# Scores taken chunk by chunk, banks held back for the next in line, and a finer clock in the planner of a linear-attention and mixing kernel

## The chip, the cores and the metric

The kernel runs on one core of one Trainium2 chip. The metric is the device time of one execution in microseconds (us). PE is the matrix engine, VectorE (DVE), ScalarE (ACT) and GpSimd (POOL) are the others. A profile is one execution; the times come from several. A quoted ratio is the mean time of one kernel's fast runs over the mean time of the fast runs of the kernel before in the same rounds, so it is not quite the ratio of the medians that stand beside it. The kernel before was timed again with every batch of experiments; its medians lay between 172.65 and 173.91 us. The changed kernel was timed once, beside the 172.69 us. So a difference in us between it and an experiment crosses batches between which the kernel before alone moved by up to 1.2 us; the ratios are the safer measure.

## The reference, cut to what matters

```python
# attention: batch 4, heads 8, sequence 768, head size 48
for t in range(S):
    cur = einsum('bhd,bhe->bhde', u * k[t], v[t])
    y[t] = einsum('bhd,bhde->bhe', r[t], state + cur)
    state = w * state + einsum('bhd,bhe->bhde', k[t], v[t])
# mixing: x is y with the heads joined, (4, 768, 384)
theta = x @ w_theta
y = einsum('ts,bsd->btd', w_tok_r, x * cos(theta)) + einsum('ts,bsd->btd', w_tok_i, x * sin(theta))
u = x + y
out = u + relu(u @ w_ch)
```

## The kernel before

The recurrence is done in chunks of 128 tokens, two chunks to a "pair", three pairs to a batch. Per pair, PE computes the scores of both chunks, VectorE masks them while it evicts them, PE forms the outputs; x, theta, sine and cosine follow. When all three pairs of a batch are there, the token mix runs: six outputs of 12 matmuls each, in four parts of three.

The kernel is not written in its final order. It declares tasks with their dependencies, engines and estimated durations, and a planner in the kernel lists them in the order of a simulated execution. The instructions are then issued in that order. Each piece of accumulator memory (PSUM) that a task needs is a token, and the planner also chooses its banks. There are 8 banks, and they are allocated as four tiles of two banks:

```python
    P = Plan(8)
    banks = [ps.tile([C, 2, 512], F32, name=f"bank{i}") for i in range(4)]

    def dbl(tok):                      # a token of two banks: a whole tile
        return banks[P.bank_of[tok] // 2]

    def bank(tok):                     # a token of one bank: half a tile
        i = P.bank_of[tok]
        return banks[i // 2][:, i % 2]
```

A token of one bank goes, if it can, beside a bank that is taken already, so that whole tiles stay free for tokens of two banks:

```python
    def pick_banks(self, acq, free, now):
        # ...
                i = min(avail, key=lambda i: ((i ^ 1) in avail, free[i]))
```

In the planner a task may start when its inputs are there, and a task's end includes a latency for the engine's pipeline, also for the next task on the same engine:

```python
                    t.end = now + ns + lat
                    # ...
                    for x in t.users:
                        x.ready = max(x.ready, t.end)
```

The token mix and its eviction, and the scores:

```python
        for t in range(2):
            to = 2 * pr + t
            tm = ("mx", b, to)
            for part in range(4):
                def mix(e, tm=tm, to=to, part=part):
                    # three matmuls into bank(tm)
                P.add({PE: pe_op(490)}, mix, ..., acq=[(tm, 1)] if part == 0 else [], ...)
            P.add({DVE: dve_op(HD)}, lambda e, ...: nc.vector.tensor_add(
                un[:, t], bank(tm)[:, :HD], x[:, to]), use=[tm], ...)
        flips(uT, [un[...] ...], ("TU", g), ...)      # six transposes on PE, then uT is evicted

        tk = [("A", g, hi) for hi in range(2)]
        # scores of both chunks: two double banks at once
        P.add({PE: pe_op(470)}, scores, rd=[kT] + rt_keys, acq=[(t, 2) for t in tk], ...)
```

## Time and profile before

| | before |
|---|---|
| median of the first 3 runs | 172.65 us (172.62 to 174.24) |
| span of the profiled run | 172.2 us |
| PE busy | 137.9 us, 80% |
| first transposes on PE | 8.80 us |
| first mixing matmul | 45.3 us |
| end of the last attention output | 138.9 us |
| mixing matmuls after that | 99 of 288 |

The page's first two parts, of the kernel before. The first line has each engine's busy time; the others are tenths of busy time and of granted clock in 40 equal slices of the span.

```profile
PE 137.9 (80%) x1491; PEld 96.1 (56%) x1491; DVE 113.2 (66%) x163; ACT 71.6 (42%) x102; POOL 76.2 (44%) x62
...
PE   3056699997969869968699999997899999699970
...
PEclk9999999999999999999969999999999999999995
```

The clock records of this run begin only at 28.47 us. Before that the row shows 9s because there is no record, not because the clock was full.

PE leads, with 34 us idle, some of it in the start and the last eviction, the rest in many short gaps.

### The profile page before, as it was taken

The numbers are of one execution on the slowest core, as the hardware profiler recorded it, in microseconds if no ns is written. First come the engines' busy times: TensorE is split into PE (matmuls) and PEld (weight loads), VectorE is DVE, ScalarE is ACT, GpSimd is POOL, SyncE is SP. The second block draws the span as 40 slices with busy tenths as digits, with TensorE's granted clock in tenths as the row PEclk, the third lists the DMA queues.
The fourth block names the chain that finished last, engine by engine and source line by source line (L and its number), as shares of the span: only waits on it lengthen the run. The fifth ranks groups of instructions, "written<-read, shape, count | busy, mean of one in ns | idle before, by whom it ended". The sixth has DMA issues, their size and how long they took to land.

```text
span 172.2 us, 3640 instructions
## 1 busy us (share of the span) xinstructions
PE 137.9 (80%) x1491; PEld 96.1 (56%) x1491; DVE 113.2 (66%) x163; ACT 71.6 (42%) x102; POOL 76.2 (44%) x62
## 2 busy tenths in 40 slices
PE   3056699997969869968699999997899999699970
PEld 1046568786745646646485657566656665455530
DVE  6274976963418897476888668646799885344361
ACT  3966236775953425457633532556105213000000
POOL 6003328079941507999799791330333332100000
PEclk9999999999999999999969999999999999999995
DMA  5999999999993399799999900220020022020222
GB/s 164 239 240 163 169 372 373 392 372 157 177 159 53 92 325 152 136 197 195 344 161 157 168 12 20 75 91 0 4 91 4 0 93 89 6 91 0 91 91 91
DMA packets 59962, 25.00 MB, mean 145 GB/s; under 512 B 50473, under 2 KB 58410, under 8 KB 59946
## 3 DMA queue, kind: packets, MB, share of 16 engines
q1 hardware_dynamic: 59920, 24.78, 65.7%
q8 instruction: 11, 0.18, 0.5%
q14 instruction: 5, 0.04, 0.1%
q10 hardware_dynamic: 26, 0.00, 0.0%
HBM read 20.06 MB, written 4.72 MB: 144 GB/s over the span
## 4 chain that ended last, share of the span: by engine, by line
PE 53%; DVE 21%; ACT 11%; issue 7%; DMA 3%; POOL 3%; ACTq 1%; DVEq 0%; POOLq 0%
PE bank L677 22%; PE bank L472 8%; PE bank L694 7%; PE bank L645 6%; DVE mAT L549 5%; ACT RT L260 5%; DVE un L683 3%; DMA wu<-in_u_dram 3%; PE bank L626 2%; DVE fin L698 2%; DVE uT L262 2%; POOL zi L658 2%; PE bank L543 2%; DVE xT L262 2%; DVE Sb L601 2%
## 5 line engine op out<-in xcount | busy, mean ns | idle before, releaser
L677 PE MATMUL bank<-zi,WiT 128*128 128x384 bf16 x144 | 29.9, 326 | 3.7 <-DVE Sb L607 1.4
L569 POOL TENSOR_TENSOR yd<-dg,vb 128x768 bf16<-128x768 f32 x12 | 17.6, 1473 | 33.1 <-ACT dg L260 33.1
L677 PE MATMUL bank<-zr,WrT 128*128 128x384 bf16 x144 | 29.6, 326 | 2.9 <-ACT RT L260 1.4
L658 POOL TENSOR_TENSOR zi<-x,sin 128x768 bf16<-128x768 bf16 x12 | 19.9, 1657 | 25.0 <-ACT sin L649 25.0
L549 DVE TENSOR_TENSOR mAT<-bank,mask 128x1024 bf16<-128x1024 f32 x24 | 29.0, 1216 | 1.0 <-PE bank L543 1.0
L519 POOL TENSOR_TENSOR Kw<-ld,wpinv 128x768 bf16<-128x768 f32 x11 | 19.8, 1822 | 11.7 <-ACT RT L260 11.7
L683 DVE TENSOR_TENSOR un<-bank,x 128x384 bf16<-128x384 f32 x24 | 13.2, 555 | 16.4 <-PE bank L677 9.4
L677 PEld LDWEIGHTS <-WiT 128*128 128x128 bf16 x144 | 13.3, 97 | 11.7 <-issue 4.6
L677 PEld LDWEIGHTS <-WrT 128*128 128x128 bf16 x144 | 13.1, 97 | 11.1 <-issue 4.2
L649 ACT ACTIVATE sin<-bank 128x768 bf16<-128x768 f32 x12 | 9.7, 811 | 20.5 <-DVE fin L698 10.6
L260 ACT ACTIVATE RT<-bank 128x768 bf16<-128x768 bf16 x16 | 12.8, 815 | 9.4 <-PE bank L472 5.5
L491 POOL TENSOR_TENSOR Rw<-r_f,wpow 128x576 bf16<-128x576 f32 x12 | 16.6, 1409 | 0.0
L698 DVE SCALAR_TENSOR_TENSOR fin<-bank,un 128x768 f32<-128x768 f32 x12 | 11.5, 956 | 6.5 <-PE bank L694 6.4
L645 PE MATMUL bank<-Wth,xT 128*128 128x384 bf16 x72 | 14.7, 343 | 1.2 <-DVE xT L262 0.9
L694 PE MATMUL bank<-Wch,uT 128*128 128x384 bf16 x72 | 13.7, 327 | 1.4 <-DVE uT L262 1.4
L633 DVE TENSOR_TENSOR x<-bank,yd 128x768 bf16<-128x768 f32 x12 | 11.4, 951 | 2.5 <-PE bank L626 1.3
L655 DVE TENSOR_TENSOR zr<-bank,x 128x768 bf16<-128x768 f32 x12 | 11.4, 950 | 1.1 <-ACT bank L652 1.1
L472 PE MATMUL bank<-ident,Rw 128*128 128x128 bf16 x96 | 8.9, 241 | 3.4 <-ACT RT L260 1.9
L260 ACT ACTIVATE vb<-ld 128x768 bf16<-128x768 f32 x12 | 10.1, 840 | 3.5 <-DMA ld<-in_v_dram 3.4
L260 ACT ACTIVATE KT<-bank 128x1024 bf16<-128x1024 bf16 x7 | 7.2, 1023 | 9.5 <-PE bank L677 4.0
L626 PE MATMUL bank<-vb,mAT 128*128 128x48 bf16 x192 | 9.6, 189 | 1.7 <-DVE mAT L549 1.6
L652 ACT ACTIVATE bank<-bank,pi 128x768 f32<-128x768 f32 x12 | 10.5, 875 | 0.0
(76 smaller groups left out, 212.3 us busy)
## 6 DMA issues: line engine op xcount, KB each, us to landing
ld<-in_k_dram SPq DMA_DIRECT2D x24, 192.0 KB, 5.3
ld<-in_v_dram SPq DMA_DIRECT2D x24, 192.0 KB, 5.2
out_dram<-fin SPq DMA_DIRECT2D x12, 384.0 KB, 2.5
r_f<-in_r_dram SPq DMA_DIRECT2D x3, 1152.0 KB, 7.8
ld<-in_moe_w_tok_r_dram SPq DMA_DIRECT2D x6, 384.0 KB, 8.6
ld<-in_moe_w_tok_i_dram SPq DMA_DIRECT2D x6, 384.0 KB, 8.2
r_f<-in_r_dram SPq DMA_DIRECT2D x2, 576.0 KB, 4.6
ld<-in_moe_w_theta_dram SPq DMA_DIRECT2D x1, 384.0 KB, 5.0
```

Of the source, the lines that this page charges most:

```text
L260: nc.scalar.activation(dst, src, Act.Copy)
L472: nc.tensor.matmul(bank16(tok)[:, i * C:(i + 1) * C], s, ident, is_transpose=True, start=(i == 0), stop=(i == n - 1))
L491: eng_of[e].tensor_mul(Rw[:, :, 2 * hp:2 * hp + 2, :D].transpose([0, 2, 1, 3]), rf[:, 2 * hp:2 * hp + 2, :].rearrange("p h (n d) -> p h n ...
L519: eng_of[e].tensor_mul(Kw[:, :, :, :D].rearrange("p a h d -> p (a h) d"), Ls[ik][:, :, :, :D].rearrange("p a h d -> p (a h) d"), wpinv.rea ...
L549: P.add({DVE: dve_op(8 * C)}, lambda e, hi=hi: nc.vector.tensor_mul(mAT[:, hi].rearrange("p a h t -> p (a h) t"), dbl(tk[hi]).rearrange("p ...
L569: P.add({POOL: pool_op(2 * HD, 1.7)}, lambda e: nc.gpsimd.tensor_mul(yd.rearrange("p a (h d) -> p (a h) d", h=H), wide(dg, D), vb.rearrang ...
L645: nc.tensor.matmul(dbl(th)[:, t, :HD], xT[:, ND * t + dk, :], Wth[:, dk, :], start=(dk == 0), stop=(dk == ND - 1))
L658: P.add({POOL: pool_op(2 * HD, 1.9)}, lambda e: nc.gpsimd.tensor_mul(zi[:, 2 * pr:2 * pr + 2], x[:, 2 * pr:2 * pr + 2], sn), rd=xk + [("si ...
L677: nc.tensor.matmul(bank(tm)[:, :HD], WT[:, so, to * C:(to + 1) * C], z[:, so], start=(part == 0 and j == 0), stop=(part == 3 and j == 2))
L683: P.add({DVE: dve_op(HD)}, lambda e, tm=tm, t=t, to=to: nc.vector.tensor_add(un[:, t], bank(tm)[:, :HD], x[:, to]), use=[tm], rd=[("x", zj ...
L694: nc.tensor.matmul(dbl(tf)[:, t, :HD], uT[:, ND * t + dk, :], Wch[:, dk, :], start=(dk == 0), stop=(dk == ND - 1))
L698: P.add({DVE: dve_op(2 * HD)}, lambda e: nc.vector.scalar_tensor_tensor(fin, dbl(tf)[:, :, :HD], 0.0, un, op0=Alu.max, op1=Alu.add), use=[ ...
```

## The change

The intent: scores of a pair need two double banks, half of all, before they can start; take one per chunk. Keep a pair of banks free for a two-bank task that is next in line. Let ScalarE share the mid-pair state. Make the planner's clock truer: PE at a lower rate in the first 25 us, GpSimd scaling slower, and no pipeline latency between two tasks of one engine. The diff, cut:

```diff
+    cold = 25000.0
-    def pick_banks(self, acq, free, now):
+    def pick_banks(self, acq, free, now, kept):
-        avail = [i for i in range(self.nbanks) if free[i] <= now]
+        avail = [i for i in range(self.nbanks) if free[i] <= now and i not in kept]
# ...
                             if g is None:
+                                if max(self.width[k] for k in t.acq) == 2:
+                                    i = min(range(0, self.nbanks, 2), key=lambda i: (
+                                        i in kept, (free[i] > now) + (free[i + 1] > now)))
+                                    kept.update((i, i + 1))
                                 continue
# ...
+                        if now < self.cold:
+                            ns *= 1.6
-                        x.ready = max(x.ready, t.end)
+                        for o in x.ready:
+                            x.ready[o] = max(x.ready[o], t.done if o == e else t.end)
# ...
+            for t in Sbs:
+                nc.vector.memset(t, 0.0)
-            opts = {POOL: pool_op(576, 2.1)}
+            opts = {POOL: pool_op(576, 2.15)}
-        opts = {POOL: pool_op(2 * HD)}
+        opts = {POOL: pool_op(2 * HD, 2.15)}
# ...
-        P.add({PE: pe_op(470)}, scores, rd=[kT] + rt_keys, acq=[(t, 2) for t in tk], ...)
-        for hi in range(2):
-            P.add({DVE: dve_op(8 * C)}, ... mAT[:, hi] ...)
+        for c in range(2):
+            tk, cc = ("A", g, c), 2 * pr + c
+            P.add({PE: pe_op(235)}, scores, rd=[kT] + rt_keys, acq=[(tk, 2)], ...)
+            P.add({DVE: dve_op(8 * C)}, ... mAT[:, c] ...)
# ...
-        P.add({DVE: dve_op(HD)}, ... Sb_mid = state * bmask ...)
+        P.add({DVE: dve_op(HD), ACT: (490, 135)}, mid, ...)   # on ACT: two 64-partition copies
```

More of the change, by code (lines that the diff above doesn't have):

```diff
@@ L26 @@
     __slots__ = ("opts", "fn", "deps", "prio", "seq", "acq", "uses", "nwait", "users", "ready",
-                 "start", "end", "mode", "lock", "eng", "name")
+                 "start", "done", "end", "mode", "lock", "eng", "name")
 class Plan:
+    cold = 25000.0
     def __init__(self, nbanks):
@@ L93, in order @@
         for t in self.tasks:
-            t.users, t.nwait, t.ready = [], len(t.deps), 0.0
+            t.users, t.nwait, t.ready = [], len(t.deps), {e: 0.0 for e in t.opts}
         for t in self.tasks:
@@ L117, in order @@
                     best, got = None, None
-                    for t in waiting[e]:
-                        if t.ready > now or (t.lock and port > now):
-                            continue
-                        if best is not None and (t.prio, t.seq) >= (best.prio, best.seq):
+                    kept = set()
+                    for t in sorted(waiting[e], key=lambda t: (t.prio, t.seq)):
+                        if t.ready[e] > now or (t.lock and port > now):
                             continue
@@ L124, in order @@
                             mine = now + t.opts[e][0]
-                            if any(max(free_at[o], now) + t.opts[o][0] < mine
+                            if any(max(free_at[o], t.ready[o], now) + t.opts[o][0] < mine
                                    for o in t.opts if o != e):
@@ L129, in order @@
                         if t.acq:
-                            g = self.pick_banks(t.acq, free, now)
+                            g = self.pick_banks(t.acq, free, now, kept)
                             if g is None:
+                                if max(self.width[k] for k in t.acq) == 2:
+                                    i = min(range(0, self.nbanks, 2), key=lambda i: (
+                                        i in kept, (free[i] > now) + (free[i + 1] > now)))
+                                    kept.update((i, i + 1))
                                 continue
                         best, got = t, g
+                        break
                     if best is None:
@@ L150, in order @@
                     t.eng, t.start = e, now
-                    free_at[e] = now + ns
+                    free_at[e] = t.done = now + ns
                     t.end = now + ns + lat
@@ L165, in order @@
             nxt = [f for f in free_at.values() if f > now]
-            nxt += [t.ready for e in ENGINES for t in waiting[e] if t.ready > now]
+            nxt += [t.ready[e] for e in ENGINES for t in waiting[e] if t.ready[e] > now]
             nxt += [f for f in free if now < f < INF]
@@ L323, in fills @@
             nc.vector.memset(bmask[Dp:, D:], 1.0)
-        P.add({DVE: (600, 100)}, fills, wr=["ones", "wu", "pi2", "uw", "bmask"], prio=-200)
+        P.add({DVE: (600, 100)}, fills, wr=["ones", "wu", "pi2", "uw", "bmask", "Sb0"], prio=-200)
         def wu_load(e):
@@ L533, in attention, with scores @@
             rd=L2(iv) + ["tables done"], wr=[kv_], prio=pb + 1, name="vcast")
-        tk = [("A", g, hi) for hi in range(2)]
-        def scores(e):
-            for c in range(2):
-                cc = 2 * pr + c
+        for c in range(2):
+            tk, cc = ("A", g, c), 2 * pr + c
+            def scores(e, tk=tk, c=c, cc=cc):
                 for hp in range(HP):
@@ L542, in scores @@
                         q = slice(hi * Dp, (hi + 1) * Dp)
-                        nc.tensor.matmul(dbl(tk[hi])[:, c, hp * C:(hp + 1) * C],
+                        nc.tensor.matmul(dbl(tk)[:, hi, hp * C:(hp + 1) * C],
                                          KT[q, c, hp, :], RT[q, hp, cc * C:(cc + 1) * C],
                                          start=(hp == 0), stop=(hp == HP - 1))
-        P.add({PE: pe_op(470)}, scores, rd=[kT] + rt_keys, acq=[(t, 2) for t in tk],
-              prio=pb + 2, mode=1, name="scores")
-        for hi in range(2):
-            P.add({DVE: dve_op(8 * C)}, lambda e, hi=hi: nc.vector.tensor_mul(
-                mAT[:, hi].rearrange("p a h t -> p (a h) t"),
-                dbl(tk[hi]).rearrange("p a (h t) -> p (a h) t", h=HP), bc(mask01, 1, 2 * HP)),
-                use=[tk[hi]], rd=["mask"], wr=[kM + (hi,)], prio=pb + 3, name="mask")
+            P.add({PE: pe_op(235)}, scores, rd=[kT] + rt_keys, acq=[(tk, 2)],
+                  prio=pb + 2, mode=1, name="scores")
+            P.add({DVE: dve_op(8 * C)}, lambda e, tk=tk, c=c: nc.vector.tensor_mul(
+                mAT[:, c].rearrange("p a h t -> p (a h) t"),
+                dbl(tk).rearrange("p a (h t) -> p (a h) t", h=HP), bc(mask01, 1, 2 * HP)),
+                use=[tk], rd=["mask"], wr=[kM + (c,)], prio=pb + 3, name="mask")
         P.add({DVE: dve_op(8 * C, 2.0)}, lambda e: nc.vector.tensor_mul(
@@ L600, in attention, with mid @@
               name="outer")
-        P.add({DVE: dve_op(HD)}, lambda e: nc.vector.tensor_mul(
-            Sb_mid, bank(tS)[:, :HD].rearrange("p (h e) -> p h e", h=HP), bc(bmask, 1, HP)),
-            use=[tS], rd=["bmask"], wr=[S_mid], prio=pb + 2.2, name="S")
+        def mid(e):
+            src = bank(tS)[:, :HD].rearrange("p (h e) -> p h e", h=HP)
+            if e == DVE:
+                nc.vector.tensor_mul(Sb_mid, src, bc(bmask, 1, HP))
+            else:
+                for hi in range(2):
+                    q, f = slice(hi * Dp, (hi + 1) * Dp), slice(hi * D, (hi + 1) * D)
+                    copy(e, Sb_mid[q, :, f], src[q, :, f])
+        P.add({DVE: dve_op(HD), ACT: (490, 135)}, mid,
+              use=[tS], rd=["bmask", "Sb0"], wr=[S_mid], prio=pb + 2.2, name="S")
         if not last:
@@ L625, in outputs @@
                 for h in range(H):
-                    nc.tensor.matmul(dbl(ty)[:, c, h * D:(h + 1) * D], mAT[:, h % 2, c, h // 2, :],
+                    nc.tensor.matmul(dbl(ty)[:, c, h * D:(h + 1) * D], mAT[:, c, h % 2, h // 2, :],
                                      vb[:, c, h * D:(h + 1) * D], start=first,
```

## The prediction

> **What bounds the kernel now.** The page gives PE 137.9 us of 172.2 (80%), VectorE 66%, ScalarE 42%, GpSimd 44%; PE has 53% of the chain of waits, VectorE 21%. PE is the limit, but it runs in program order and waits behind evictions. The planner inside the kernel fixes that order, so PE's idle time is what a better plan can win. Read from PE's timeline, as sums of gaps: 8.8 us before the first transposes, about 7 more to 46 us; about 4.8 (46 to 75), 4.5 (75 to 100), 2.6 (100 to 125), 3.3 (125 to 167); then 5 us of last eviction and store. In the 80 to 90 us stretch the granted clock is 0.83, and 16 score matmuls take 1.04 us instead of 0.62: about 1.5 us lost.
>
> Until about 27 us PE issues 384-column matmuls every 0.32 us, later every 0.164. The Trainium skill ("TensorE: Matmul & The Clock Gate", Part 1) describes a half-rate start; the trace agrees on the ratio, though the slow stretch is much longer than its 3.4 us window.
>
> **The change.** PE's arithmetic stays. (1) Scores of a pair needed two double banks at once (4 of 8 banks), until their 1.22 us masks; now each chunk takes one, so scores start with less room. (2) A blocked double-bank task reserves a pair, so singles no longer starve it. (3) The plan knows the cold clock and slower GpSimd scaling (1822 ns measured; the old plan reckoned 1552), and adds no latency to same-engine handovers. (4) The mid-pair state may go to ScalarE as two 64-partition copies; the built order sends 7 of 12 there. VectorE saves 7 x 0.55 = 3.9 us; ScalarE gains, estimated from its 768- and 1024-element copies (815 and 1023 ns), 7 x 2 x 0.35 = 4.9 us. (5) Four memsets at the start, estimated 0.1 to 0.2 us each, mostly hidden behind the 4.75 us u load.
>
> The built order shows more: batch 0's third yd precedes the second zi on GpSimd, so the 1.3 us PE wait at 39 us should go; token-weight transposes move behind batch 0's attention; attention of the last batch is packed, leaving 129 instead of 99 mixing matmuls after its last output, which fill the 1.2 us PE stall at 146 us.
>
> **How much counts.** Perhaps 2 of the 7 us before 46 us, 2 of 4.8, 2 of 4.5 with some of the cold 1.5, 0.5 of 2.6, and 1 of 3.3: 7 to 8 us. Against it: the start slips 0 to 0.5 us; packed attention leans on VectorE with fewer mixing matmuls between, and reserved banks idle: new waits of 3 to 4 us. Net about -4.
>
> **Predicted:** 168.4 us, 165.0 to 172.3. Faster by over 2%: 0.54; within 2%: 0.39; slower by over 2%: 0.07.
>
> **What would show it.** PE busy near 137 us, idle down from 34 to about 30; the last attention output ends near 129 us (139 before) with no PE gap over 0.7 us between it and the last mixing; mixing begins near 43.5 us (45.5); VectorE near 109 us, ScalarE near 76, its half copies near 0.35 us; masks near 1.2 us; granted clock 1.0 in every middle stretch. Wrong steps: PE waits on the mask grow in the last batch, or the mix's wait for RT evictions at 47 us stays.
>
> **What would make it wrong.** The planner's durations differ from the chip's, so its tighter order can stall where the old one had slack (slower); or freed banks remove nearly all middle gaps (under 165). If every gap merely moves, the time stays within 1%.

## More of the kernel before

The start, from the timeline of the kernel before (start, duration, engine, line, operation, out<-in; in brackets the idle time before it and what ended that):

```profile
3.87 0.49 ACT L365 ACTIVATE lw_f<-bank 128x384 f32<-128x384 f32 x1 [1.23 <-DVE tok_f L339]
...
4.39 3.14 ACT L369 ACTIVATE wpow<-lw_f,tok_f 128x384 f32<-128x384 f32 x6
...
7.05 0.24 PE L377 MATMUL bank<-ident_f,wu 8*128 8x8 f32 x1 [3.22 <-DMA wu<-in_u_dram]
...
7.90 2.10 DVE L491 TENSOR_TENSOR Rw<-r_f,wpow 128x576 bf16<-128x576 f32 x3
...
8.80 0.80 PE L472 MATMUL bank<-ident,Rw 128*128 128x128 bf16 x6 [1.51 <-DVE Rw L491]
```

The decay powers wpow are computed on ScalarE while the load of u is still under way. The token mix near the end, same view: VectorE evicts a finished mix (un) while PE works on the next one.

```profile
152.56 0.65 PE L677 MATMUL bank<-zr,WrT 128*128 128x384 bf16 x3
...
153.04 0.65 PE L677 MATMUL bank<-zi,WiT 128*128 128x384 bf16 x3
...
153.53 1.14 PE L677 MATMUL bank<-zr,WrT 128*128 128x384 bf16 x6
154.22 0.56 DVE L683 TENSOR_TENSOR un<-bank,x 128x384 bf16<-128x384 f32 x1 [1.39 <-PE bank L677]
...
154.51 0.67 PE L472 MATMUL bank<-ident,un 128*128 128x128 bf16 x6
```

All that PE waited for from the last attention output on (waits of PE in the window 139 to 172 us: total us, times, longest):

```profile
PE bank L677 <- DVE un L683: 1.3, 2, 1.2
PE bank L694 <- DVE uT L262: 1.0, 3, 0.7
PE bank L472 <- DVE un L683: 0.3, 1, 0.3
PE bank L677 <- DVE uT L262: 0.2, 1, 0.2
```

## The result, and the profile after

The changed kernel took 182.15 us (median of 4 runs, 181.13 to 182.72) against 172.69 us; the ratio of the fast runs is 1.0524, 95% interval 1.0457 to 1.0591. It is 5% slower, outside the predicted range.

The page's first two parts, of the changed kernel:

```profile
PE 139.6 (77%) x1491; PEld 97.5 (54%) x1491; DVE 111.3 (62%) x162; ACT 74.8 (41%) x115; POOL 74.3 (41%) x61
...
PE   3035879899898878788997988965798878878760
...
PEclk9999999999999999999999999999569999999997
```

PE's busy time rose only by 1.7 us; its idle time rose from 34 to 41 us, and the last quarter of the row shows 7s and 8s where the kernel before had 9s. The start, from the timeline:

```profile
2.46 1.61 PE L373 MATMUL bank<-w_row,ones 1*128 1x384 f32 x2 [2.46 <-DVE bmask L334]
...
7.13 0.24 PE L388 MATMUL bank<-ident_f,wu 8*128 8x8 f32 x1 [3.06 <-DMA wu<-in_u_dram]
...
7.41 0.49 ACT L376 ACTIVATE lw_f<-bank 128x384 f32<-128x384 f32 x1 [4.76 <-PE bank L388]
...
7.93 3.14 ACT L380 ACTIVATE wpow<-lw_f,tok_f 128x384 f32<-128x384 f32 x6
...
11.11 1.43 DVE L502 TENSOR_TENSOR Rw<-r_f,wpow 128x576 bf16<-128x576 f32 x2 [2.64 <-ACT wpow L380]
...
12.01 1.23 PE L483 MATMUL bank<-ident,Rw 128*128 128x128 bf16 x10 [4.64 <-DVE Rw L502]
```

The logarithm lw_f needs only the broadcast of w, which PE had finished at 4.07 us (L373). It now waits for the little matmul on w and u (L388), whose result it does not read, and the first transposes start 3.2 us later. The mixing tail, from the timeline:

```profile
165.27 1.14 PE L693 MATMUL bank<-zi,WiT 128*128 128x384 bf16 x6
...
166.24 0.65 PE L693 MATMUL bank<-zr,WrT 128*128 128x384 bf16 x3
166.93 0.56 DVE L699 TENSOR_TENSOR un<-bank,x 128x384 bf16<-128x384 f32 x1 [1.48 <-PE bank L693]
167.54 0.65 PE L693 MATMUL bank<-zr,WrT 128*128 128x384 bf16 x3 [0.65 <-DVE un L699]
...
168.03 0.50 PE L483 MATMUL bank<-ident,un 128*128 128x128 bf16 x6
...
168.36 0.65 PE L693 MATMUL bank<-zi,WiT 128*128 128x384 bf16 x3
169.05 0.56 DVE L271 COPY uT<-bank 128x768 bf16<-128x768 bf16 x1 [1.56 <-PE bank L693]
169.66 0.65 PE L693 MATMUL bank<-zi,WiT 128*128 128x384 bf16 x3 [0.65 <-DVE uT L271]
```

A mix is done at 166.24. Its eviction un waits for the three matmuls of the *next* mix, and that mix's second part waits for the eviction. The matmuls read zr, zi and the weights, not un. The same happens with uT, and it happens in each pair of the tail. What PE waited for from the last attention output on (window 135 to 176 us):

```profile
PE bank L693 <- DVE un L699: 3.2, 5, 0.7
PE bank L693 <- DVE uT L271: 2.9, 5, 0.6
PE bank L710 <- DVE uT L271: 0.7, 1, 0.7
PE bank L483 <- DVE un L699: 0.7, 1, 0.7
PE bank L661 <- DVE xT L271: 0.2, 1, 0.2
```

The first two lines, 6.1 us, are mixing matmuls that wait for evictions they have nothing to do with. Before, such waits came to 1.5 us.

**What they wait for.** The built program lists, per instruction, the semaphore counts that it waits for. Two lines from it for one pair of the tail (line, out<-in, first column of the output in its tile, and what the wait is for, looked up by its count):

```
L693 bank0<-zr1,WrT  columns from 512, waits for VectorE 156: un0 <- bank0, columns from 0
L693 bank0<-zi1,WiT  columns from 512, waits for VectorE 157: uT0 <- bank0, columns from 0
```

Columns 0 to 511 and 512 to 1023 are the two banks of one tile. The two instructions touch no common bank. They touch the same tile. I call such a wait a *neighbour wait*. I classed every wait in the two built programs in this way: the waited-for instruction shares no SBUF tile and no bank with the waiter, but shares a PSUM tile. Then I added up the PE gaps over 0.15 us in the trace by the class of the wait that ended them. The kernel before has 42 neighbour waits on PE, and such waits ended 10.3 us of gaps. The changed kernel has 46, with 18.9 us; the start's lost 3.2 us are not among them, since that wait is ScalarE's. The other gaps are 19.0 and 16.9 us, the start included. The same wait can be harmless or not: it costs only when it ends last.

The same sums by stage (all PE gaps over 0.15 us, and neighbour waits in brackets):

| | first transposes | first mix | last attention output ends | mixing matmuls left then | gaps to 28 us | 28 us to last output | after it |
|---|---|---|---|---|---|---|---|
| before | 8.8 | 45.3 | 138.9 | 99 | 12.2 | 14.3 (6.7) | 2.7 (1.5) |
| changed | 12.0 | 45.9 | 134.9 | 129 | 13.7 | 14.3 (11.1) | 7.7 (6.1) |

The last attention output does end 4 us earlier, but with 30 more mixing matmuls to come. At the 0.164 us from start to start that dense mixing shows, these are 4.9 us of work, and the chains that go with them are more. The changed kernel had won nothing by then, and lost the rest after it. From 28 us to the last output the gaps from other waits did shrink, from 7.6 to 3.2 us, but the neighbour waits grew by as much.

### The profile page after: what moved, and what is told of

Its sections match the earlier page's. It is cut to its first block, busy times and chain, and to the rows that moved or that the text cites. A ratio compares the mean times of both kernels' runs of the same rounds, so it can differ in the third digit from the quotient of the medians.

```text
span 180.8 us, 3651 instructions
## 1 busy us (share of the span) xinstructions
PE 139.6 (77%) x1491; PEld 97.5 (54%) x1491; DVE 111.3 (62%) x162; ACT 74.8 (41%) x115; POOL 74.3 (41%) x61
## 4 chain that ended last, share of the span: by engine, by line
PE 63%; DVE 16%; ACT 11%; issue 5%; DMA 3%; ACTq 0%; DVEq 0%
PE bank L693 26%; PE bank L483 9%; PE bank L661 7%; PE bank L710 7%; PE bank L466 5%; DVE un L699 4%; PE bank L642 3%; DMA wu<-in_u_dram 3%; ACT xT L269 2%; DVE uT L271 2%; ACT RT L269 2%; PE bank L637 2%; ACT wpow L380 2%; ACT KT L269 2%; DVE mAT L558 2%
## 5 line engine op out<-in xcount | busy, mean ns | idle before, releaser
L693 PE MATMUL bank<-zr,WrT 128*128 128x384 bf16 x144 | 30.5, 329 | 7.4 <-DVE un L699 5.3
L674 POOL TENSOR_TENSOR zi<-x,sin 128x768 bf16<-128x768 bf16 x12 | 19.6, 1641 | 25.7 <-ACT sin L665 18.9
L699 DVE TENSOR_TENSOR un<-bank,x 128x384 bf16<-128x384 f32 x24 | 13.3, 556 | 21.9 <-PE bank L693 16.8
L530 POOL TENSOR_TENSOR Kw<-ld,wpinv 128x768 bf16<-128x768 f32 x10 | 18.1, 1818 | 14.5 <-DMA ld<-in_k_dram 14.5
L661 PE MATMUL bank<-Wth,xT 128*128 128x384 bf16 x72 | 15.4, 358 | 1.2 <-ACT Sb L269 0.7
L269 ACT ACTIVATE RT<-bank 128x768 bf16<-128x768 bf16 x16 | 12.1, 821 | 8.3 <-DVE un L699 5.6
L710 PE MATMUL bank<-Wch,uT 128*128 128x384 bf16 x72 | 13.7, 326 | 0.7 <-DVE uT L271 0.7
L671 DVE TENSOR_TENSOR zr<-bank,x 128x768 bf16<-128x768 f32 x12 | 11.4, 954 | 2.3 <-ACT bank L668 2.3
L483 PE MATMUL bank<-ident,Rw 128*128 128x128 bf16 x96 | 8.0, 242 | 6.2 <-DVE Rw L502 4.6
L661 PEld LDWEIGHTS <-xT 128*128 128x128 bf16 x72 | 7.2, 104 | 6.6 <-issue 2.2
L553 PE MATMUL bank<-RT,KT 64*128 64x128 bf16 x192 | 9.4, 234 | 1.8 <-DVE KT L271 0.8
L483 PEld LDWEIGHTS <-Rw 128*128 128x128 bf16 x96 | 6.9, 109 | 6.9 <-issue 5.9
```

The source lines that it names most:

```text
L269: nc.scalar.activation(dst, src, Act.Copy)
L483: nc.tensor.matmul(bank16(tok)[:, i * C:(i + 1) * C], s, ident, is_transpose=True, start=(i == 0), stop=(i == n - 1))
L530: eng_of[e].tensor_mul(Kw[:, :, :, :D].rearrange("p a h d -> p (a h) d"), Ls[ik][:, :, :, :D].rearrange("p a h d -> p (a h) d"), wpinv.rea ...
L661: nc.tensor.matmul(dbl(th)[:, t, :HD], xT[:, ND * t + dk, :], Wth[:, dk, :], start=(dk == 0), stop=(dk == ND - 1))
L674: P.add({POOL: pool_op(2 * HD, 1.9)}, lambda e: nc.gpsimd.tensor_mul(zi[:, 2 * pr:2 * pr + 2], x[:, 2 * pr:2 * pr + 2], sn), rd=xk + [("si ...
L693: nc.tensor.matmul(bank(tm)[:, :HD], WT[:, so, to * C:(to + 1) * C], z[:, so], start=(part == 0 and j == 0), stop=(part == 3 and j == 2))
```

## The experiments

Each experiment ran beside the kernel before. All gave correct results. One run each of b4, e4 again, scores only, aware and "named, dealt" was slow: the medians include it, the ratios do not. Theory A: waits are recorded per tile of two banks, and the changed order puts pieces that are alive at the same time into one tile. Rival B: the packed attention and the shorter distance between a mix and its consumers leave PE with real latency.

| run | what | median us | ratio to before, 95% interval |
|---|---|---|---|
| e1 | changed, tail in other banks | 175.05 | 1.0079 (1.0034 to 1.0123) |
| e2 | changed, one start token in another bank | 179.88 | 1.0358 (1.029 to 1.0427) |
| e5 | both | 173.01 | 0.9979 (0.9937 to 1.0022) |
| e3 | changed, all banks dealt again, careless | 181.43 | 1.0447 (1.0387 to 1.0507) |
| b3 | before, the same | 183.73 | 1.0571 (1.0525 to 1.0617) |
| e4 | changed, all banks dealt again, with care | 165.37 | 0.9523 (0.9476 to 0.9569) |
| b4 | before, the same | 164.64 | 0.945 (0.9368 to 0.9533) |
| e4 again | beside the next | 166.17 | 0.9565 (0.9526 to 0.9603) |
| b4 again | beside the last | 163.36 | 0.9427 (0.9394 to 0.946) |
| e6 | changed, latency within an engine back | 175.85 | 1.0121 (1.0069 to 1.0174) |
| e7 | before, without that latency | 178.48 | 1.0287 (1.0236 to 1.0338) |
| scores only | before, chunked scores alone | 174.2 | 1.0024 (0.995 to 1.0097) |
| scores only, dealt | | 167.07 | 0.9633 (0.9561 to 0.9704) |
| aware | changed, planner that knows the rule | 167.09 | 0.9562 (0.9468 to 0.9656) |
| no cold | changed, cold clock not modelled | 188.67 | 1.0864 (1.0817 to 1.0911) |
| named | changed, cold and zero latency undone | 179.58 | 1.0373 (1.0328 to 1.0418) |
| no cold, dealt | | 172.91 | 0.995 (0.9905 to 0.9995) |
| named, dealt | | 173.74 | 0.9991 (0.9924 to 1.0057) |

### Same order, other banks: the tail

The planner runs unchanged. After it, and before anything is issued, banks are dealt out again to chosen tokens. A search keeps the assignment in which two tokens that are alive together and share a tile cost the least planned waiting. I compared the built programs: on every engine the sequence of operations is the same, only the banks differ.

```diff
-    for t in P.order():
+    out_of = P.order()
+    since = max(n for n, t in enumerate(out_of) if t.name == "y")   # the last attention output
+    P.rebank(out_of, lambda k, n: n > since)
+    for t in out_of:
         t.fn(t.eng)
# in rebank, for two tokens a, b in one tile:
+                    p, q = (x, y) if n < m else (y, x)          # tasks of a and b, in issue order
+                    if p.eng != q.eng and (PE in (p.eng, q.eng) or "cos" in (p.name, q.name)):
+                        s += max(0.0, p.end - q.start)
```

> The changed kernel, same instruction order on every engine; only the PSUM banks of the pieces that start after the last attention output are dealt out again, so that two pieces alive at once share a two-bank tile less often. Theory A (the build records waits per two-bank tile, so a matmul group waits for an eviction of the neighbour bank): the nine PE gaps of 0.65 us in the last 40 us mostly go, the stretch from the last attention output to the end of the span falls from 45.9 to 40 us, the time from 182.15 to about 176.5 us. Rival B (the packed order leaves too few matmuls between a mix and the transposes of its result, so the gaps are real latency): the gaps stay, the stretch stays above 44 us, the time above 181 us.

Measured: 175.05 us, 7.1 less than the changed kernel. From the last attention output to the end of the span 38.8 us (134.2 to 173.0) instead of 45.9. The waits of PE in that stretch (134 to 168.5 us):

```profile
PE bank L776 <- DVE uT L337: 0.7, 1, 0.7
PE bank L549 <- DVE un L765: 0.6, 1, 0.6
PE bank L727 <- DVE zr L737: 0.6, 1, 0.6
PE bank L759 <- DVE xT L337: 0.2, 1, 0.2
```

No mixing matmul (L759) waits for un or uT any more. The timeline of the same step as above:

```profile
153.89 1.14 PE L759 MATMUL bank<-zi,WiT 128*128 128x384 bf16 x6
...
154.87 1.14 PE L759 MATMUL bank<-zr,WrT 128*128 128x384 bf16 x6
155.07 0.56 DVE L765 TENSOR_TENSOR un<-bank,x 128x384 bf16<-128x384 f32 x1 [0.99 <-PE bank L759]
...
155.84 0.50 PE L549 MATMUL bank<-ident,un 128*128 128x128 bf16 x6
...
156.18 1.14 PE L759 MATMUL bank<-zi,WiT 128*128 128x384 bf16 x6
```

The same six matmuls between a mix and the transposes of its result now cover the eviction, since it starts 0.2 us after the mix and not after half of the next one. From one group of such transposes to the next it is 5.21 us (155.84 to 161.05), where the changed kernel took 6.83 (161.20 to 168.03). Theory A holds for the tail, and B falls there: the order was not the trouble. (The profiled span shrank by 7.8 us, 0.8 of it before the tail, where no bank had changed: there the clock records begin at 24.5 us and not at 31.8, a difference between executions.)

### Same order, one other bank: the start

```diff
+    P.rebank(out_of, lambda k, n: k == "wu")     # the token of the w/u matmul
```

> The changed kernel, with one piece (the transposed u and w) moved to a bank of another tile, nothing else. Theory A: the ScalarE logarithm no longer waits for the w/u matmul in the neighbour bank, the first transposes of r start near 8.9 instead of 12.0 us. How much of the 3.1 us reaches the end is open: A expects part of it to be absorbed before the mixing starts (45.95 us), time 179 to 182 us. Rival C (the start slip carries through): the whole 3 us, 179 us.

Measured: 179.88 us, 2.3 less. ScalarE's logarithm starts at 3.86 again and the first transposes at 8.65, from the timeline:

```profile
3.86 0.49 ACT L441 ACTIVATE lw_f<-bank 128x384 f32<-128x384 f32 x1 [1.22 <-DVE tok_f L415]
...
6.91 0.24 PE L453 MATMUL bank<-ident_f,wu 8*128 8x8 f32 x1 [3.08 <-DMA wu<-in_u_dram]
...
8.65 1.44 PE L548 MATMUL bank<-ident,Rw 128*128 128x128 bf16 x12 [1.51 <-DVE Rw L567]
```

The two results lay in the two banks of one tile. In the kernel before they did too, but there the logarithm was issued ahead of the matmul. Of the 3.4 us won at the first transposes, 2.3 reach the end (2.9 by the ratios).

### Both together

```diff
+    P.rebank(out_of, lambda k, n: n > since or k == "wu")
```

> The changed kernel with both small repairs, the tail's banks and the bank of the transposed u and w. If the two losses add up (7.1 and 2.3 us, measured one by one), the time is 172.8 us, within 1% of the kernel before; if the start's gain is absorbed further on, 174 to 175 us.

Measured: 173.01 us, ratio 0.9979. In us the two losses add up (7.1 and 2.3 against 9.1 measured); by the ratios, 4.5% and 1.7% against 5.5%. Together they are the whole distance to the kernel before. What the change meant to win in the middle came to nothing.

### All banks dealt again, carelessly: a miss, and a lesson

```diff
+    P.rebank(out_of, lambda k, n: True)
```

> The changed kernel, same order, with all pieces dealt out to banks again so that neighbours in a tile rarely wait for each other (waits of PE on the other bank of a tile: 46 in the program before, 8 now). Theory A: PE idle falls by 10 us or more, the time to 168 to 173 us. Rival B: 177 us or more, since the packed attention waits on VectorE whatever the banks.

> The kernel before, same order, all pieces dealt out to banks again in the same way (42 waits of PE on the other bank of a tile, now 12). Theory A: the kernel before carries about 11 us of such gaps after the start too, so it also gains, to 167 to 171 us. Rival B: within 1% of 172.7 us.

Measured: 181.43 and 183.73 us, both far off. Neighbour waits did nearly vanish (1.1 and 1.2 us of PE gaps), but gaps from real waits rose, from 16.9 to 32.0 us in the changed order and from 19.0 to 33.5 in the order before. The mistake was mine. The dealing counted a bank as free as soon as its last eviction had been *issued*, so the next user was put where the eviction was still to run. A stretch of the timeline of e3 shows score matmuls and transposes waiting for masks in their own bank:

```profile
94.07 0.40 PE L618 MATMUL bank<-RT,KT 64*128 64x128 bf16 x8 [0.65 <-DVE mAT L623]
...
95.78 0.61 PE L548 MATMUL bank<-ident,Kw 128*128 128x128 bf16 x8 [0.55 <-DVE mAT L623]
```

### All banks dealt again, with the planned end of an eviction respected

```diff
         toks = sorted(first, key=lambda k: first[k])
+        # a bank counts as taken until the plan has its last eviction done
+        for k in toks:
+            n = last[k]
+            while n + 1 < len(out) and begin[n + 1] < ends[k]:
+                n += 1
+            last[k] = n
```

> The changed kernel, same order, all pieces dealt out to banks again, now with a bank counted as taken until the plan has its last eviction done (the run that dealt out all banks before reused them as soon as the eviction had been issued, and its PE waits for reuse of the same bank rose from 17 to 32 us). Waits of PE on the other bank of a tile in the program: 26, against 46. Theory A: PE gaps from the other bank fall from 18.9 us to 8 or less without a rise of the others, and the time to 168 to 173 us. Rival B (what is left is VectorE's packed attention): as the tail-only run or worse, 174.5 us or more.

> The kernel before, same order, banks dealt out again with the planned end of an eviction respected (waits of PE on the other bank of a tile: 23 in the program, against 42). Theory A (such waits tax both orders, and the changed order is the better one once they are gone): 167.5 to 171 us, above the 165.4 us of the changed order. Rival D (the dealing is the whole gain and the change has none): 164 to 166.5 us.

Measured: 165.37 us for the changed order, 16.8 less than with its own banks, and 164.64 for the order before. Both are below the ranges that theory A gave. Gaps from neighbour waits fell to 6.6 and 3.3 us; the others came to 17.8 (16.9 with the old banks) and 22.5 (19.0). Both orders carried this tax, so my expectation that the changed order would be the better one without it failed, and the rival D, that the dealing is the whole gain, came nearer. To settle it, both ran again side by side, in five rounds:

> The changed order with banks dealt out again, a second time, now beside the order before dealt the same way, on one chip: is the changed order better or worse once both are free of most waits on the other bank? So far 0.952 against 0.945 of the kernel before, from different rounds. If the order matters: over 1% apart, without overlap of the intervals. If not: within 1%.

> The order before, dealt the same way, beside the run above: 163 to 166 us; within 1% of it if the changed order is worth nothing.

Measured: 166.17 and 163.36 us, ratios 0.9565 and 0.9427, intervals apart. Without most neighbour waits the changed order is the slower one, by about 1.5% (0.9565 / 0.9427). Why is not isolated: the profiled run of e4 again also shows 13.7 us at half clock after its first full record, that of b4 again 3.4. The order before with its banks dealt again is the fastest kernel and beats both kernels. Its page begins:

```profile
PE 133.5 (83%) x1491; PEld 94.3 (58%) x1491; DVE 113.7 (70%) x163; ACT 71.4 (44%) x102; POOL 76.5 (47%) x62
```

Its gaps over 0.15 us come to 23.3 us, 6 less than the kernel before, while it is about 10 us faster. The rest shows as 4.4 us less PE busy time (133.5 against 137.9) for the same 1491 matmuls. One part shows in the clock records: they begin, at full clock, at 21.3 us here and at 28.5 in the kernel before, and until then matmuls come at about half the pace. How much of the 4.4 us that explains I did not isolate.

### Which part of the change moved neighbours together

> The changed kernel with one part undone: the planner adds the pipeline's latency again to handovers within one engine, as before the change. Theory A1 (the zero latency made the planner run a token mix's four parts back to back, so that the next mix starts in the neighbour bank while the finished one is being evicted): the plan interleaves two mixes again, the tail's 0.65 us gaps mostly go (8 such waits in the tail of the program, against 11), time 174 to 178 us. Rival A2 (another part of the change made the tail share tiles): still 180 us or more.

```diff
-                            x.ready[o] = max(x.ready[o], t.done if o == e else t.end)
+                            x.ready[o] = max(x.ready[o], t.end)
```

Measured: 175.85 us, 6.3 less than the changed kernel. Neighbour gaps after the last output fell from 6.1 to 1.0 us.

> The kernel before with that one part alone: no latency within one engine. A1: it shows the tail's 0.65 us gaps and loses 2 to 6 us (175 to 179 us). A2: within 1% of the kernel before, 172 to 174 us.

The edit is the same, the other way round, in the kernel before. Measured: 178.48 us, 2.9% slower. Neighbour gaps after the last output rose from 1.5 to 3.2 us, and those in the middle from 6.7 to 11.4. So A1 holds. With a latency of 215 ns between the four parts of a mix, the plan fills the time with another mix's part. Without it the plan runs the four parts in a row. When a mix ends, its bank is still taken, and the bank picker then prefers exactly its neighbour for the next mix. In the kernel before, the two interleaved mixes mostly lay in different tiles, so PE had matmuls of the other one to issue while an eviction ran. That was luck: nothing in its plan aimed at it.

> The kernel before with the scores taken chunk by chunk, one double bank each, and nothing else of the change. If the named part of the change is good by itself: 168 to 171 us. If it too shifts the mixing tail into shared tiles (7 such waits after the last attention output in the program, 4 before, 11 in the changed kernel): 173 to 177 us.

The edit: the scores block, the mask and the index of mAT from the diff above, in the kernel before. Measured: 174.2 us, ratio 1.0024, inside the second range (173 to 177). One of its four runs, the profiled one, was slow, so its trace is not used; whether shared tiles in the tail hide a gain is therefore not shown. The part that gave the change its name is worth nothing measurable here.

> The same with the banks dealt out again. Theory A: at or below the kernel before dealt the same way, 165 to 169 us; chunked scores worth 1 to 3 us then.

Measured: 167.07 us, ratio 0.9633. Within the range, but not at or below the order before dealt the same way (0.945 in the same batch). Chunked scores gain nothing there either: they are 1.9% slower, with the intervals apart.

> The changed kernel with a planner that knows the rule: no task is planned while another engine works in the other bank of its tile (no such wait left in the tail of the program, 22 in all). Theory A: 163 to 168 us, as good as the dealing. If planning around the rule costs banks: 168 to 172 us.

```diff
+    def clash(self, t, e, now, i, width):
+        mine = set(range(i, i + width))
+        return any(x.end > now and x.eng != e and not mine & b
+                   and (PE in (e, x.eng) or "cos" in (t.name, x.name))
+                   for x, b in self.log[i // 2])
# a task that would clash isn't started, and a bank that would clash isn't picked
```

Measured: 167.09 us, within the range. A planner told of the rule turns the same change from a loss of 5% into a gain of 4%, though the order before with dealt banks stays better.

### Undoing the planner's parts: they don't add up

> The changed kernel without the cold clock in the plan alone. In its built order the ScalarE logarithm comes before the w/u matmul again, although both are in one tile. If the cold model made the start slip: the first transposes start near 8.9 us, the time 179 to 181 us, the tail's 0.65 us gaps stay. If the start stays at 12.0 us, the cold model was not the cause.

```diff
-    cold = 25000.0
+    cold = 0.0
```

Measured: 188.67 us, 6.5 *more*. The first transposes did start at 8.8 us, so the cold model is what moved the start. But every other task was planned anew as well: neighbour gaps were 18.4 us, about those of the changed kernel, and the other gaps rose from 16.9 to 20.9.

> The changed kernel without two of its quiet planner parts: latency within an engine is added again, and the cold clock is not modelled. The chunked scores, the held-back banks, the slower GpSimd figure and the mid-pair state on ScalarE stay. If the loss sits in the two quiet parts (6.3 us measured for the latency; 2.3 us for the start): 172 to 175 us, the named parts worth nothing. If the named parts gain once the quiet ones are gone: below 171 us. If they cost: above 177 us.

Both edits together. Measured: 179.58 us, above the range expected if the loss sat in the two quiet parts alone. Neighbour gaps after the last output are 0.6 us. Its gaps over 0.15 us (30.6 us) are about those of the kernel before (29.2), yet it is 6 us slower. Its granted clock was 0.945 to 0.960 in all four runs, against 0.979 to 0.994 of the kernel before in that batch.

> The order of the changed kernel without the cold model (188.67 us), same order, banks dealt out again (waits of PE on the other bank of a tile in the program: 15, against 52). If the spread between planner variants is the tile waits: 164 to 169 us, as the other dealt orders. If the order itself is bad: above 175 us.

> The order with only the named parts of the change (179.58 us), same order, banks dealt out again (22 such waits, against 47). If the spread is the tile waits: 164 to 169 us. If the named parts cost by themselves (its gaps above 0.15 us were no larger than those of the kernel before, its granted clock was lower): above 171 us.

The same two orders with their banks dealt again: 172.91 and 173.74 us. The dealing takes 15.8 and 5.8 us off, so neighbour waits are a large part of the spread. But the first ends between the ranges that I gave and the second in the upper one (above 171 us, the named parts cost by themselves). Both are 8 to 10 us above the order before dealt again (164.64 and 163.36), so the orders differ in worth as well. Their neighbour gaps, 3.7 and 5.6 us against 3.6 in b4 again, do not explain that. Their profiled runs show 13.7 and 23.9 us at half clock after the first full record, against 3.4. Whether the clock is a cause or follows from the orders' own gaps is left open. I can't attribute time to a single planner part beyond the pairs e6 and e7, since each edit plans everything anew.

## Why the prediction was wrong, point by point

- **The step that failed** is in "How much counts": "new waits of 3 to 4 us. Net about -4". The prediction costed each bank as if it were independent and never asked what a wait is recorded for. The neighbour waits of the new order cost 7.1 us in the tail (e1) and 2.3 us in the start (e2). With both repaired, the ratio is 0.9979 (e5): the expected "7 to 8 us" of gains, less other costs, came to about nothing. By the traces they were there as shorter waits of other kinds (7.6 to 3.2 us from 28 us to the last output), but neighbour waits grew by the same 4.4 us in that stretch. Nor do they appear when most neighbour waits are gone from both orders: there the changed order is 1.5% slower (e4 again and b4 again), and the cause of that stays open.
- **"129 instead of 99 mixing matmuls after its last output, which fill the 1.2 us PE stall at 146 us."** The 129 came true and the stall went. But ten waits for un and uT took its place, 6.1 us in all, 0.65 each in the repeating pattern. The warning sign that I named, a gap over 0.7 us, did not show; many gaps just below it did the damage. A sum would have been the right test.
- **"The start slips 0 to 0.5 us."** It slipped 3.2 us at the first transposes. The four memsets were cheap (0.22 us each); the swap of two issues on one tile was not looked for. The built order showed it, on ScalarE and PE, and the prediction overlooked it.
- **"The last attention output ends near 129 us."** It ended at 134.9. "Mixing begins near 43.5": 45.9. Moving one token's bank (e2) gave 43.4 and 132.4.
- **Right:** the 1.3 us wait at 39 us went; masks stayed at 1.22 us; the half copies on ScalarE took 0.32 us (0.35 estimated), seen in the group line of the changed kernel below; ScalarE's busy time was 74.8 us (76 predicted). VectorE's was 111.3 (109), so less than half of the saving came, and PE's 139.6 (137), where it rose and did not fall. The work was costed to within 3 us, the waiting was not.

```profile
L269 ACT ACTIVATE Sb<-bank 64x192 bf16<-64x192 f32 x14 | 4.5, 324 | 9.2 <-PE bank L595 4.5 <-PE bank L693 3.4 <-DVE un L699 1.2
```

- **"Granted clock 1.0 in every middle stretch"** was wrong too. In the packed attention of the last batch PE waits again and again, and the clock drops. Stretches of the changed kernel (busy time of PE, PEld, DVE, ACT, POOL, then granted clock):

```profile
120.00:130.00 10.00, 5.69 (x81) 3.97 (x80) 8.41 (x10) 3.31 (x7) 1.48 (x1) 0.87 0.00 0
130.00:140.00 10.00, 9.47 (x111) 6.58 (x110) 6.04 (x9) 3.12 (x5) 4.98 (x4) 0.79 0.01 2
```

PE is busy for 5.69 of 10 us, then six theta matmuls take 2.08 us instead of 1.14. The Trainium skill, "TensorE: Matmul & The Clock Gate", section "A second HAM failure mode: psum-queue depth-cycling", describes a PE that idles briefly between groups of matmuls often enough to be throttled. The trace agrees with that picture in part: no gap from 120 to 130 us is over 1.11 us, but PE was busy for only 1.55 of the 3.41 us before the clock fell to half at 127.33 us, where it stayed to 134.16. It fell once in this stretch and did not swing. That these gaps caused the drop is argued, no run isolates it.

The prediction's own doubt, "its tighter order can stall where the old one had slack", pointed the right way, but it named the planner's durations as the reason. The runs show another one: a rule of the build that the planner does not know. One direct test was not run: declaring eight tiles of one bank, with the order and the banks left alone. It would need the two-bank tokens split.

## What to carry to other kernels

Waits are recorded for what the program declares, not for what the hardware needs: in these programs two independent results in the two banks of one tile wait for each other in both directions. If a kernel chooses its own banks, look in the built program for waits whose two ends share a tile but no bank, and sum the gaps behind them before tuning the order. When an order changes, ask which independent pieces become neighbours in memory, and judge a tail by the sum of its small gaps, not by the longest.

## What the Trainium skill lacked or had wrong

- "PSUM — Partial Sum Buffer", section "Terms", gives the bank, per quadrant, as the unit in which two engines must not meet. It says nothing of waits that a build records for a larger unit. Here tiles of two banks made pieces in different banks wait for each other: 7.1 us in the tail and 2.3 us at the start (e1, e2), and dealing the banks again made the kernel before 5.7% faster (b4 again, ratio 0.9427). No page has this.
- "TensorE: Matmul & The Clock Gate", Part 1, gives a warm-up of about 3.4 us of sustained work, but not how busy "sustained" has to be. Here 384-column matmuls still came every 0.32 us at 25 to 27 us in the kernel before (six in 2.10 us), every 0.164 us later, and the changed kernel had the slow rate at 28 us too (six in 2.10 us). This does not contradict the page. The clock records begin at 28.47 and 31.76 us, with the full clock, and the matmuls speed up there. In the 3.41 us before those times PE was busy for 3.23 and 3.41 us. In the 3.41 us before that it was busy for 3.17 and 2.44, and the slow rate went on. The profile view prints 1.00 where there is no record.
